# Keys and queries of the later head pairs: through a scratch in device memory into float32r tiles, and transposed as float32r

## The chip, the cores and the metric

The kernel runs on one core of one Trainium2 chip. The core has five engines with instruction streams of their own: PE (matrix products, with its weight loads listed as PEld), DVE, ACT, POOL and SP; in this kernel SP issues nearly all transfers. Each engine takes its instructions in the order of the program and waits on semaphores for the others. The metric is device microseconds for one execution, lower is better; the time quoted is the median of several runs.

## The reference, cut to what matters

The program is an attention block and two dense blocks behind it. Only the first is touched here.

```python
# q, k, v: (2, 8, 768, 64) float32, proj: (64, 6)
q_bits = (np.einsum('bhsd,dk->bhsk', q, proj) > 0).astype(np.int64)
k_bits = (np.einsum('bhsd,dk->bhsk', k, proj) > 0).astype(np.int64)
q_bucket = np.sum(q_bits * powers, axis=-1)
k_bucket = np.sum(k_bits * powers, axis=-1)
mask = q_bucket[:, :, :, None] == k_bucket[:, :, None, :]
scores = scale * np.matmul(q, k.transpose(0, 1, 3, 2))
scores = np.where(mask, scores, -1000000000.0)
attn = softmax(scores)                       # written out in the original
x = np.matmul(attn, v)                       # -> (1536, 512) tokens
x = np.maximum(np.maximum(x @ w1, x @ w2), x @ w3) @ w_out
out = gelu_sigmoid(x @ w_in) @ w_out2        # widths 2048 and 512
```

## The kernel before, in words

The 16 heads are taken as 8 pairs `g` (two heads of one batch side by side). For each pair the kernel loads k, q and v (`load_raw`, tiles `raw`, three buffers), and brings k and q into a layout with the feature on the partition by transposing 128x128 blocks on PE against an identity (`prep_transpose`, L293, into a PSUM tile `T`): 2 tensors x 2 halves x 3 blocks, 12 transposes for a pair. ACT and DVE split each transposed half into a high and a low float32r part (`kq`: L302 to L310). Four products of `kq` with the projection give the bucket bits (`prep_bits`, L319; `aug`), and eight transfers per head put it all together as `kst` and `qst` (`prep_stack`, L343).

The first pair goes another way (`load_first`, `solo_transpose` L363, `solo_bits` L392 and L394), with tiles of its own and transposes with 64 columns of weights. `solo_bits` needs `pds`, which DVE makes from `proj` (tile `pf`, loaded by ACT's queue in L1303) in L1312 to L1320.

Then each of 96 units `u` (128 queries of a head) goes through scores (L425, tile `S`), clamp and row minimum on DVE (L432, tile `se`), exponential on ACT (L438), the reciprocal of the sum (L442), scaling on POOL (L448), transposition on PE in float32 (L457), a high and a low part (L463, L467) and the product with v (L475, `PV`). The result is moved by three small transfers (`xm`, `xt`: L500 to L503) and added and split on POOL (L508 to L518). After that come the dense blocks (L681 to L1212), whose products are in float32r.

The order on every engine in the attention part is set by `plan`: a list of tasks with a due time (`u` plus `DUE`), dependencies, buffers taken and given, and an engine with an occupancy and a latency from `COST`. SP is planned like an engine; its kinds are `raw`, `stack`, `xm`, `xm2` and `wraw`. `filled` puts products on zeros (L1483) into PE's gaps of the plan in the first part. The planned order is then enforced on each engine (`in_order`).

Of the kernel before, what the change touches and what calls it, by code (L numbers as in the profile page):

```python
# [201 lines left out]
def build(tc, q, k, v, proj, w1, w2, w3, w_out, m2_in, m2_out, out):  # L202
# [16 lines left out]

    sb_all = tc.tile_pool(name="sb", bufs=1)  # L220
    sb = sb_all.__enter__()
    sb_att = tc.tile_pool(name="sb_att", bufs=1)
    at = sb_att.__enter__()
    ps_att = tc.tile_pool(name="ps_att", bufs=1, space=bass.MemoryType.PSUM)
# [4 lines left out]
    def st(shape, tag, bufs, dtype=F32, pool=None):  # L229
        seq[0] += 1  # L230
        if pool is None:
            pool = sb if tag in shared else at
        return pool.tile(shape, dtype, tag=tag, name=f"{tag}_{seq[0]}", bufs=bufs)
# [21 lines left out]
        nc.tensor.matmul(wps[:, :512], warm[:, :P], warm, start=True, stop=True)  # L255
    ident = st([P, P], "ident", 1)
    make_identity(nc, ident)
    off = st([NR, 1], "off", 1)
    nc.gpsimd.memset(off, 0.0)
    for n, base in enumerate((70, 64, 50, 44, 38, 18, 12, 6)):  # L260
# [16 lines left out]
    stacks = {}  # L277
    vstack = {}

    def load_raw(g, what):  # L280
        b, p = divmod(g, NPAIR)
        for name, src in (("k", k), ("q", q), ("v", v)):
            if name in what:
                t = st([P, NTILE, 2, D], "raw", 3)
                for j in range(2):
                    nc.sync.dma_start(t[:, :, j, :], src[b, 2 * p + j].rearrange("(p c) d -> p c d", c=NTILE))
                qkv_raw[g, name] = t

    def prep_transpose(g, name, a, get):
        t = qkv_raw[g, name]  # L290
        pst = get()
        for c in range(3):
            nc.tensor.transpose(pst[:, c * P:(c + 1) * P], t[:, 3 * a + c].rearrange("p j d -> p (j d)"), ident)  # L293
        if a == 0:
            kq[g, name] = (st([P, S], "kq", 4, F32R), st([P, S], "kq", 4, F32R))
        s = slice(a * HALF, (a + 1) * HALF)
        hi, lo = (x[:, s] for x in kq[g, name])
        o = pst[:, :HALF]

        def on_act():  # L300
            if name == "k":
                nc.scalar.copy(hi, o)  # L302
            else:
                nc.scalar.activation(hi, o, AF.Copy, scale=QSCALE)

        def on_dve():
            if name == "k":
                nc.vector.tensor_tensor(out=lo, in0=o, in1=f32(hi), op=ALU.subtract)
            else:
                nc.vector.scalar_tensor_tensor(out=lo, in0=o, scalar=QSCALE, in1=f32(hi),  # L310
                                               op0=ALU.mult, op1=ALU.subtract)
        return on_act, on_dve
# [979 lines left out]
    if True:  # L1292
# [46 lines left out]
        def task(kind, u, fn, name=None, deps=(), take=(), give=(), cost=None):  # L1339
            tasks.append((u + DUE[kind], len(tasks), fn, name, deps, take, give, COST[cost or kind]))  # L1340
# [17 lines left out]
        task("pd1", 0, project_high, ("pdth",), deps=[("pdf",)], cost="high")  # L1358
        task("pd1", 0, project_low, ("pdt",), deps=[("pdth",), ("sp", 0, 3)], cost="low")
        task("raw", -36, lambda: load_raw(0, "v"), ("r0", "v"))  # L1360
        task("S", -99, lambda: None, ("PE", "warm"), cost="warm")
        task("v", -2, lambda: prep_v(0, 0), ("vs", 0, 0), deps=[("r0", "v")])
        for g in range(NG):
# [4 lines left out]
            task("v", u0, lambda g=g: prep_v(g, 1), ("vs", g, 1), take=("vs",), deps=[("vs", g, 0)],  # L1368
                 give=("rv",))
            if g + 1 < NG:  # L1370
                task("raw", u0, lambda g=g: load_raw(g + 1, "k"), ("rk", g + 1), take=("rk",))
                task("raw", u0, lambda g=g: load_raw(g + 1, "q"), ("rq", g + 1), take=("rq",))
                task("raw", u0 + 8, lambda g=g: load_raw(g + 1, "v"), ("rv", g + 1), take=("rv",))
                task("v", u0 + 9, lambda g=g: prep_v(g + 1, 0), ("vs", g + 1, 0), take=("vs",), deps=[("rv", g + 1)])
                for n in range(6):
# [110 lines left out]
            t[2]()  # L1486
        ps_att.__exit__(None, None, None)
        sb_att.__exit__(None, None, None)
        moe_jobs()
        in_order(first)  # L1490
    sb_all.__exit__(None, None, None)
# [29 lines left out]
```

## Time and profile before

| what | value |
|---|---|
| median of 3 runs | 674.24 us (674.07 to 674.43) |
| the profiled execution, its time | 674.57 us |
| its span, from the first to the last instruction | 672.8 us |
| PE busy | 666.1 us (99%) |
| DVE busy | 570.1 us (85%) |
| ACT busy | 438.3 us (65%) |
| POOL busy | 320.2 us (48%) |

The span is 1.8 us shorter than the time of the same execution, and that execution is 0.33 us above the median. Busy time of PE counts overlapping products as one stretch and includes the draining of each, so PE at 99% is not PE at its peak: how long a product occupies PE is read from the distance between starts.

### The profile page before, as it was taken

How to read it: one execution, taken by the hardware profiler on the slowest of the kernel's cores; microseconds unless marked ns; L12 is line 12 of the kernel's file. 1: busy time of each engine (PE TensorE's matmuls, PEld its weight loads, DVE VectorE, ACT ScalarE, POOL GpSimd, SP SyncE). 2: the span in 40 equal slices, each digit the busy share in tenths (PEclk: the TensorE clock that was granted, in tenths of full speed). 3: DMA queues.
4: the chain of work that ended last, by engine and by line, in shares of the span. 5: the costliest groups of instructions: out<-in, count | busy, mean ns of one | idle time of the engine just before them, and what ended most of it. 6: DMA issues, size and time to landing. Idle time of an engine off the chain costs nothing.

```text
span 672.8 us, 11441 instructions
## 1 busy us (share of the span) xinstructions
PE 666.1 (99%) x3931; PEld 586.6 (87%) x3933; DVE 570.1 (85%) x1052; ACT 438.3 (65%) x882; POOL 320.2 (48%) x425
## 2 busy tenths in 40 slices
PE   8999999999999999999999999999999999999998
PEld 6899999999999988888888888888888888888886
DVE  8999988999999859999998878886878878787945
ACT  6999989899999835455554554787363736546360
POOL 7476777887887743723433052222333434242400
PEclk9999999999999999999999999999999999999999
DMA  4767578676846112222222132131312130212005
GB/s 117 158 150 174 133 167 195 153 179 139 197 111 144 29 47 64 63 63 64 63 90 67 48 111 93 34 96 62 95 45 80 63 95 31 94 33 94 33 1 188
DMA packets 73690, 64.96 MB, mean 97 GB/s; under 512 B 38608, under 2 KB 64464, under 8 KB 73632
## 3 DMA queue, kind: packets, MB, share of 16 engines
q1 hardware_dynamic: 73408, 64.10, 36.2%
q8 instruction: 31, 0.51, 0.3%
q14 instruction: 27, 0.22, 0.1%
q10 hardware_dynamic: 224, 0.13, 0.1%
HBM read 38.80 MB, written 3.15 MB: 62 GB/s over the span
## 4 chain that ended last, share of the span: by engine, by line
PE 89%; DVE 3%; POOL 3%; DMA 2%; issue 1%; ACT 1%; POOLq 0%; SPq 0%; ACTq 0%
PE acc L902 33%; PE acc L1201 19%; PE PV L475 8%; PE T L457 7%; PE S L425 7%; PE acc L1061 7%; PE acc L681 4%; PE T L681 1%; DVE se L432 1%; POOL se L448 1%; PE T L319 1%; DMA xm<-xt 1%; PE T L293 1%; DVE ptl L467 1%; DMA xt<-xt 1%
## 5 line engine op out<-in xcount | busy, mean ns | idle before, releaser
L594 POOL TENSOR_SCALAR wmag<-wmag 128x512 f32<-128x512 f32 (+1 forms) x58 | 45.9, 792 | 122.5 <-ACT wmag L587 122.1
L467 DVE TENSOR_TENSOR ptl<-T,pth 128x512 fp32r<-128x512 f32 x144 | 93.9, 684 | 8.2 <-ACT pth L463 7.8
L448 POOL TENSOR_SCALAR se<-se,rc 128x768 f32<-128x768 f32 x96 | 87.2, 919 | 20.7 <-DVE rc L442 17.2
L432 DVE TENSOR_SCALAR_CACHE_REDUCE se<-S 128x768 f32<-128x768 f32 x96 | 90.3, 948 | 3.8 <-PE S L425 3.4
L438 ACT ACTIVATE se<-se,mn 128x768 f32<-128x768 f32 x96 | 91.1, 951 | 2.3 <-DVE se L432 2.2
L425 PE MATMUL S<-kst,qst 128*128 128x512 f32 (+3 forms) x384 | 87.7, 354 | 0.2 <-DVE se L432 0.2
L463 ACT CAST pth<-T 128x512 fp32r<-128x512 f32 x144 | 78.0, 592 | 5.9 <-PE T L457 4.9
L457 PE MATMUL T<-ident,se 128*128 128x128 f32 x576 | 77.5, 273 | 1.3 <-POOL se L448 0.6
L1201 PE MATMUL acc<-wolo,gh 128*128 128x512 f32 (+1 forms) x194 | 75.0, 387 | 0.0
L1201 PE MATMUL acc<-wohi,gh 128*128 128x512 f32 (+1 forms) x194 | 75.0, 387 | 0.0
L475 PE MATMUL PV<-pth,vst 128*128 128x256 f32 x288 | 73.6, 290 | 0.0
L475 PE MATMUL PV<-ptl,vst 128*128 128x256 f32 x288 | 71.2, 282 | 0.0
L457 PEld LDWEIGHTS T<-ident,se 128*128 128x128 f32 x576 | 65.6, 140 | 4.3 <-POOL se L448 1.1
L1209 DVE TENSOR_TENSOR res<-acc,res 128x512 f32<-128x512 f32 (+1 forms) x85 | 57.3, 682 | 11.1 <-PE acc L1201 9.0
L425 PEld LDWEIGHTS S<-kst,qst 76*128 76x128 f32 (+1 forms) x384 | 59.0, 190 | 6.3 <-DVE se L432 1.4
L1201 PE MATMUL acc<-wohi,gl 128*128 128x512 f32 (+1 forms) x194 | 59.3, 387 | 0.0
L622 POOL TENSOR_TENSOR wlo<-wmag,whi 128x512 fp32r<-128x512 f32 (+1 forms) x28 | 37.8, 1350 | 39.8 <-ACT whi L617 39.7
L475 PEld LDWEIGHTS PV<-pth,vst 128*128 128x128 f32 x288 | 54.7, 190 | 1.3
L475 PEld LDWEIGHTS PV<-ptl,vst 128*128 128x128 f32 x288 | 54.9, 191 | 0.0
L902 PE MATMUL acc<-xl,whi 128*128 128x256 f32 (+1 forms) x150 | 47.1, 327 | 0.0
L902 PE MATMUL acc<-xh,whi 128*128 128x256 f32 (+1 forms) x150 | 46.9, 326 | 0.0
L617 ACT CAST whi<-wmag 128x512 fp32r<-128x512 f32 (+1 forms) x42 | 25.3, 601 | 27.3 <-DVE wmag L612 24.0
(236 smaller groups left out, 1724.1 us busy)
## 6 DMA issues: line engine op xcount, KB each, us to landing
wraw<-in_moe_w_dram SPq DMA_DIRECT2D x18, 512.0 KB, 4.4
wraw<-in_moe_w_in_dram SPq DMA_DIRECT2D x16, 512.0 KB, 3.8
wraw<-in_moe_w_out_dram SPq DMA_DIRECT2D x16, 512.0 KB
kst<-kq SPq DMA_DIRECT2D x42, 192.0 KB, 3.5
qst<-kq SPq DMA_DIRECT2D x42, 192.0 KB, 3.5
raw<-in_k_dram SPq DMA_DIRECT2D x16, 192.0 KB, 3.2
raw<-in_q_dram SPq DMA_DIRECT2D x16, 192.0 KB, 3.8
raw<-in_v_dram SPq DMA_DIRECT2D x16, 192.0 KB, 4.2
```

The lines of the kernel that those rows point to most:

```text
L425: nc.tensor.matmul(pss[:, x], qs[r, k, c * P:(c + 1) * P], ks[r, k, x], start=k == 0, stop=k == 1)
L432: nc.vector.tensor_scalar(out=se[u], in0=pss[:, :S], scalar1=1.0e9, scalar2=None, op0=ALU.min, op1=ALU.min, accum_out=mn[u])
L438: nc.scalar.activation(se[u], se[u], AF.Exp, bias=mn[u], scale=-1.0, accum_out=sm[u // 2][:, u % 2:u % 2 + 1])
L448: nc.gpsimd.tensor_scalar(out=se[u], in0=se[u], scalar1=rc[u // 2][:, u % 2:u % 2 + 1], scalar2=1.0, op0=ALU.mult, op1=ALU.mult)
L457: nc.tensor.transpose(pst[:, i * P:(i + 1) * P], se[2 * jq + o][:, c * P:(c + 1) * P], ident)
L463: nc.scalar.copy(ptr[jq][0][:, n * 512:(n + 1) * 512], tps[jq, n])
L467: nc.vector.tensor_tensor(out=ptr[jq][1][:, s], in0=tps[jq, n], in1=f32(ptr[jq][0][:, s]), op=ALU.subtract)
L475: nc.tensor.matmul(pv[jq], vs[:, c, :], ptr[jq][t].rearrange("p (o c n) -> p c o n", o=2, c=NTILE)[:, c], start=(c == 0 and t == 0), stop= ...
L902: nc.tensor.matmul(o, w[:, c], x[:, c], start=first and m == 0, stop=m == len(turns) - 1, skip_group_check=True)
L1061: nc.tensor.matmul(o, w[:, c % 3, :], h[:, s], start=(c == 0 and z == 0), stop=(c == FT - 1 and z == 2))
L1201: nc.tensor.matmul(o, g[:, s], w.rearrange("p c f -> p (c f)")[:, e], start=n == 0, stop=n == len(turns) - 1)
L1209: nc.vector.tensor_tensor(out=res[t][:, e], in0=o, in1=res[t][:, e], op=ALU.add)
```

## The change

A pool in device memory is opened (`dr_att`), and for pairs 1 to 7 a new task `move_raw` copies k and q (2 heads, 384 KB each) from the input to a scratch tile there, two buffers for each name. `load_raw` then reads k and q from the scratch, into a `raw` tile that is declared float32r (the bits are those of the float32 input). v is loaded as before. The transposes of `prep_transpose` take this tile and a float32r copy of the identity, `identr`, and write PSUM through a float32r view. The first pair and the transposes of L457 stay float32. The costs in `COST` and the due times in `DUE` are unchanged.

```diff
     sb = sb_all.__enter__()
+    dr_att = tc.tile_pool(name="dr_att", bufs=1, space=bass.MemoryType.DRAM)
+    dr = dr_att.__enter__()
...
     make_identity(nc, ident)
+    identr = st([P, P], "identr", 1, F32R)
+    nc.scalar.copy(identr, ident)
...
+    def move_raw(g):
+        b, p = divmod(g, NPAIR)
+        for name, src in (("k", k), ("q", q)):
+            moved[g, name] = dr.tile([2, S, D], F32, tag="moved" + name, name=f"moved_{name}{g}", bufs=2)
+            nc.sync.dma_start(moved[g, name], src[b, 2 * p:2 * p + 2])
...
-                t = st([P, NTILE, 2, D], "raw", 3)
+                t = st([P, NTILE, 2, D], "raw", 3, F32 if name == "v" else F32R)
                 for j in range(2):
-                    nc.sync.dma_start(t[:, :, j, :], src[b, 2 * p + j].rearrange("(p c) d -> p c d", c=NTILE))
+                    x = src[b, 2 * p + j] if name == "v" else moved[g, name][j]
+                    nc.sync.dma_start((t if name == "v" else f32(t))[:, :, j, :], x.rearrange("(p c) d -> p c d", c=NTILE))
...
-            nc.tensor.transpose(pst[:, c * P:(c + 1) * P], t[:, 3 * a + c].rearrange("p j d -> p (j d)"), ident)
+            nc.tensor.transpose(pst[:, c * P:(c + 1) * P].bitcast(F32R), t[:, 3 * a + c].rearrange("p j d -> p (j d)"), identr)
...
+        task("raw", -35, lambda: move_raw(1), ("moved", 1))
...
-                task("raw", u0, lambda g=g: load_raw(g + 1, "k"), ("rk", g + 1), take=("rk",))
-                task("raw", u0, lambda g=g: load_raw(g + 1, "q"), ("rq", g + 1), take=("rq",))
+                task("raw", u0, lambda g=g: load_raw(g + 1, "k"), ("rk", g + 1), take=("rk",), deps=[("moved", g + 1)])
+                task("raw", u0, lambda g=g: load_raw(g + 1, "q"), ("rq", g + 1), take=("rq",), deps=[("moved", g + 1)])
+                if g + 2 < NG:
+                    task("raw", u0 + 7, lambda g=g: move_raw(g + 2), ("moved", g + 2))
```

The first place is the beginning of ACT's program, which the copy of the identity enters. Before (`pf` is the tile for `proj`, `kst` the first high part of pair 0):

```order
L1303 DMA pf_95<-in_proj_dram 64x6
L370 ACT_TABLE_LOAD
L370 CAST kst_109<-T_130 64x384
L370 CAST kst_109<-T_134 64x384
L372 ACTIVATE qst_110<-T_139 64x384
```

And with the change (L383 and L385 are the old L370 and L372):

```order
L261 ACT_TABLE_LOAD
L261 CAST identr_79<-ident_74 128x128
L1316 DMA pf_99<-in_proj_dram 64x6
L383 CAST kst_113<-T_134 64x384
L383 CAST kst_113<-T_138 64x384
```

The table load and the copy of the identity now stand ahead of the issue of the transfer of `proj`, which was ACT's first work.

The second place is SP in the middle of the attention part, where v of pair 4 and k and q of pair 5 are loaded. Before (`xm` and `xt` are the small moves of a result, `wraw` a block of dense weights):

```order
L503 DMA xt_336_1440<-xt_380_1627 64x256
L286 DMA raw_1690<-in_v_dram 128x6x64 x2
L568 DMA wraw_1710<-in_moe_w_dram 128x4x256
L286 DMA raw_1727<-in_k_dram 128x6x64 x2
L502 DMA xm_1503<-xt_413_1742 64x256
L503 DMA xt_352_1502<-xt_413_1742 64x256
L286 DMA raw_1774<-in_q_dram 128x6x64 x2
```

And with the change (L299 loads into `raw`, L290 fills the scratch, L515 and L516 are the old L502 and L503):

```order
L516 DMA xt_337_1463<-xt_381_1650 64x256
L299 DMA raw_1713<-in_v_dram 128x6x64 x2
L581 DMA wraw_1733<-in_moe_w_dram 128x4x256
L290 DMA moved_k_1743<-in_k_dram 16x6144
L290 DMA moved_q_1745<-in_q_dram 16x6144
L299 DMA raw_1772<-moved_k_1184 128x6x64 x2
L515 DMA xm_1526<-xt_413_1766 64x256
L516 DMA xt_353_1525<-xt_413_1766 64x256
```

Two transfers of 384 KB for a later pair stand in front of the load of k and of the small moves `xm` and `xt`.

The third place is PE at the start, around the first transposes of pair 1 (`S` is a tile of scores, `L392` and `L394` are bits of pair 0, `warm` is filling). Before:

```order
L394 MATMUL T_242<-kst_111,pds_98 76x384
L293 MATMUL T_247<-ident_72,raw_179 128x128 x3
L425 MATMUL S_255<-kst_109,qst_110 128x512
L425 MATMUL S_255<-kst_109,qst_110 128x256
L425 MATMUL S_255<-kst_109,qst_110 128x512
L425 MATMUL S_255<-kst_109,qst_110 128x256
L293 MATMUL T_265<-ident_72,raw_179 128x128 x3
L392 MATMUL T_273<-kst_111,pds_98 76x384
```

And with the change, up to the first of them (five fills, of which two rows stand here):

```order
L438 MATMUL S_264<-kst_113,qst_114 128x256
L405 MATMUL T_278<-qst_116,pds_102 76x384
L407 MATMUL T_278<-qst_116,pds_102 76x384
L405 MATMUL T_282<-qst_116,pds_102 76x384
L407 MATMUL T_282<-qst_116,pds_102 76x384
L1499 LDWEIGHTS warm_66
L1499 MATMUL PV_205<-warm_66 128x512
L306 MATMUL T_301<-identr_79,raw_222 128x128 x3
```

The transposes of k of pair 1 come after the fourth tile of scores, the last bits of pair 0 and five fills, no longer around the fourth tile of scores; the transposes of q of pair 1 follow behind the fifth and the sixth tile.

## Rows read from the trace of the kernel before

**Rows 1.** The page: span, busy time of each engine.

```profile
span 672.8 us, 11441 instructions
PE 666.1 (99%) x3931; PEld 586.6 (87%) x3933; DVE 570.1 (85%) x1052; ACT 438.3 (65%) x882; POOL 320.2 (48%) x425
```

**Rows 2.** Chain of waits, first 40 us: start, length, engine, line, count.

```profile
21.61 1.42 PE T L319 x8
...
28.45 1.43 PE PV L475 x12
29.89 1.31 PE T L457 x12
...
36.07 1.41 PE S L425 x8
```

**Rows 3.** Line L293: count, duration in ns (min/median/max), first and last start.

```profile
L293 PEld LDWEIGHTS T<-ident,raw x84: 137/140/143, 12.5 to 187.1; 128*128 128x128 f32 x84
L293 PE MATMUL T<-ident,raw x84: 270/272/328, 12.7 to 187.2; 128*128 128x128 f32 x84
```

**Rows 4.** Stretches: length, busy PE, PEld, DVE, ACT, POOL, PEclk, DMA share, GB/s.

```profile
150.00:200.00 50.00, 48.83 (x372) 46.37 (x371) 47.62 (x102) 46.60 (x100) 41.75 (x60) 1.00 0.64 149
```

**Rows 5.** The same view as rows 4, one stretch of the start.

```profile
20.00:30.00 10.00, 10.00 (x70) 9.20 (x71) 10.00 (x24) 9.32 (x20) 4.30 (x7) 1.00 0.79 172
```

**Rows 6.** Line L319, the same columns as for L293.

```profile
L319 PEld LDWEIGHTS T<-kq,pdt x56: 186/188/192, 21.3 to 190.3; 128*128 128x128 f32 x56
```

**Rows 7.** Timeline of PE: start, length, line, out<-in, weights, moving operand, count.

```profile
11.32 0.49 PE L363 MATMUL T<-ident,raw 128*64 128x128 f32 x3
...
12.70 0.49 PE L293 MATMUL T<-ident,raw 128*128 128x128 f32 x3
```

**Rows 8.** Timeline of ACT at the start; in brackets the idle time before and its end.

```profile
0.80 0.55 ACTq L1303 DMA_DIRECT2D pf<-in_proj_dram  x1
1.39 1.28 ACT L370 ACT_TABLE_LOAD   x1 [1.39 <-PEq L1506]
4.25 0.47 ACT L370 CAST kst<-T 64x384 fp32r<-64x384 f32 x1 [1.58 <-PE T L363]
...
10.07 0.30 ACT L1330 CAST pdt<-pdf 128x128 fp32r<-128x128 f32 x1
```

**Rows 9.** Timeline of POOL at the start.

```profile
1.07 0.29 POOL masks.py:199 TENSOR_SCALAR_AFFINE_SELECT ident<-ident 128x128 f32<-128x128 f32 x1
```

**Rows 10.** Timeline of DVE at the start.

```profile
3.44 0.17 DVE L1312 COPY pf<-pf 64x6 f32<-64x6 f32 x1 [0.62 <-DMA pf<-in_proj_dram]
...
4.75 1.19 DVE L381 TENSOR_TENSOR kst<-T,kst 64x384 fp32r<-64x384 f32 x2 [0.20 <-ACT kst L370]
...
16.04 1.02 DVE L308 TENSOR_TENSOR kq<-T,kq 128x384 fp32r<-128x384 f32 x2
```

**Rows 11.** Timeline of SP's queue at the start: issues of transfers, start and length.

```profile
7.94 1.23 SPq L286 DMA_DIRECT2D raw<-in_k_dram  x2
...
27.03 0.86 SPq L343 DMA_DIRECT2D qst<-aug  x1
```

**Rows 12.** The page, transfers: count, KB of one, us from issue to landing.

```profile
wraw<-in_moe_w_dram SPq DMA_DIRECT2D x18, 512.0 KB, 4.4
...
kst<-kq SPq DMA_DIRECT2D x42, 192.0 KB, 3.5
```

**Rows 13.** Timeline of SP's queue, the second place of the change.

```profile
101.68 0.64 SPq L568 DMA_DIRECT2D wraw<-in_moe_w_dram  x1
...
103.77 2.19 SPq L502 DMA_DIRECT2D xm<-xt  x1
```

**Rows 14.** Timeline of POOL behind it.

```profile
108.91 0.74 POOL L508 TENSOR_TENSOR xt<-xt,xm 128x256 f32<-128x256 f32 x1 [2.23 <-DMA xt<-xt]
```

**Rows 15.** Groups by line: count, busy us, mean ns, idle before and its ends.

```profile
L508 POOL TENSOR_TENSOR xt<-xt,xm 128x256 f32<-128x256 f32 x24 | 18.2, 756 | 11.0 <-DMA xm<-xt 6.0 <-DMA xt<-xt 4.3
```

More of the change, by code (lines that the diff above doesn't have):

```diff
@@ L278, in build @@
     vstack = {}
+    moved = {}
+    def move_raw(g):
[3 more added lines that the diff above has]
+            nc.sync.dma_start(moved[g, name], src[b, 2 * p:2 * p + 2])
     def load_raw(g, what):
@@ L1488, in build @@
         sb_att.__exit__(None, None, None)
+        dr_att.__exit__(None, None, None)
         moe_jobs()
```

## The prediction

> **What bounds the kernel now.** The page comes first: PE is busy for 666.1 of 672.8 us [rows 1], so nothing is short that PE does not do. Busy time of PE counts overlap, so I read next, in the chain of waits, how far apart PE's instructions start: 12 transposes of L457 take 1.31 us, 109 ns each; 12 products of 256 columns (L475) 1.43 us, 119 ns each; 8 products of 384 columns (L319) 1.42 us, 178 ns each [rows 2]. These are pieces in which PE follows PE without a gap. The 84 transposes that the change touches have the same form as those of L457 (272 ns for one, drained) and run from 12.5 to 187 us [rows 3]; at 109 ns they hold PE for 9.2 us, 1.4% of the span. That is the whole stock from which a gain can come.
>
> Then the stretches, for who stands next to PE. From 150 to 200 us DVE is busy for 47.6 of 50 us, ACT for 46.6, POOL for 41.8 [rows 4]. A shorter PE soon meets DVE and ACT there. From 20 to 30 us DVE is busy for all of 10.0 us [rows 5]: at the start DVE sets the pace, and PE has fills in its order. So a gain of PE counts only behind the start, and a delay of DVE at the start counts in full. The attention part is where all edits are; the dense blocks behind it are PE's alone and only begin earlier or later.
>
> **The transposes.** The trace has no float32r product with 128 moving columns. From below: a float32r product costs 119 ns at 256 columns and 178 at 384 [rows 2], 59 for 128 columns, so the line gives 60 ns at 128; that saves 49 ns of 109. From above: the weights of a float32r product with 128 columns load for 188 ns [rows 6], those of the float32 transpose for 140 [rows 3]. If the longer load sets the pace, the nearest row with such loads is L475 with 119 ns, 10 ns worse than now. No row is near either end, since this is a transpose in one respect and a float32r product in the other; I take 85, halfway between 60 and the present 109, a saving of 24. The 12 transposes of pair 1 lie at the start, where DVE sets the pace; 72 are left: 72 x 24 ns = 1.7 us. DVE and ACT are busy for 95 and 93% beside them [rows 4], so I let a quarter go to waits on these: **-1.3 us**, with ends at -3.5 (72 x 49 ns, nothing given back) and +0.7 (72 x 10).
>
> Here the Trainium skill speaks against the change. What the trace shows first: three transposes with 64 columns of weights (L363) take 0.49 us, and three with 128 columns (L293) 0.49 us as well [rows 7]; half the weights bought nothing, so in float32 it is the moving side that sets 109 ns. The Trainium skill, "TensorE: Matmul & The Clock Gate", section "LDWEIGHTS (loading the stationary operand)", has a load last by its count of columns, which for 128 gives 107 ns (an estimate by that page's formula). By that rule a row of transposes with 128 columns of weights would stand at its 109 ns in either type, the term would be zero and the sum +2.1; the 64-column rows do not agree with it for float32, and no row shows it for a float32r transpose. Its case is a rival below.
>
> **The start.** The copy `identr` is put ahead of the issue of the transfer of `proj` on ACT. Before, that issue began at 0.80 us and the table load ran from 1.39 to 2.67 [rows 8]; `ident` was ready at 1.36 [rows 9]. DVE waited for `proj` until 3.44 [rows 10], 2.64 us after the issue. Now ACT begins at 0.80 with the table load (1.28 us, to 2.08), and copies the identity; a cast of 128x128 on ACT lasts 0.30 [rows 8], so the issue begins at about 2.4 and DVE has `proj` at 5.0 instead of 3.44: 1.6 us later. Behind that wait stand the little instructions of `pds`, and L381 at 4.75, which had waited 0.20 us for ACT [rows 10]: DVE's chain up to L381 moves from 4.55 to 6.1, and L381 begins **1.4 us** later. ACT's own copy costs nothing: ACT had been waiting for PE until 4.25 [rows 8]. From L381 on DVE works without a pause until 31 us (its timeline; the last ten of these us are in [rows 5]), so the 1.4 us are handed on to the clamps and from there to PE. Ends: 2.0 if the table load stays at 1.39 (issue at 3.0), and 0.4 if the new order gives 1.0 back: the `kq` pair of L308, 1.02 us [rows 10], no longer stands ahead of the clamp of the fourth tile of scores, so the first reciprocal comes that much earlier. I take **+1.4**: the work is only put off, and DVE has it all before the stretch ends.
>
> The first loads: k of pair 1 was issued at 7.94 [rows 11], when its buffer came free. Now SP must first see the scratch written. Four transfers of 384 KB go out from 4 us on; one of 512 KB lands after 4.4 us [rows 12], so the first is there at about 8.5 and costs nothing, but the other three, 1152 KB, are queued ahead of the load. Between the rows of 192 and of 512 KB lie 320 KB and 0.9 us [rows 12], so 1152 KB are some 3.2 us, and the landing goes from about 12 to 15. PE reaches these transposes behind five fills at about 16 us. `kst` and `qst` of pair 1 go out some 3 us later than before; their last issue ended at 27.9 [rows 11], with 3.5 us to land [rows 12] that is 31.4, and the first tile of scores that needs them (the thirteenth in PE's order) began at 36.07 [rows 2]. The cover is 4.7 us; without it the 3 us would count. I take nothing.
>
> **SP and the transfers in the middle.** Each of the pairs 4 to 7 brings two issues on SP (0.6 us each by the `wraw` issue [rows 13], 1.2 us together), mostly where SP waited for a result to move. More counts what is queued behind: at the second place shown, the 768 KB stand ahead of the load of k and of `xm` and `xt`. There already before, with `wraw` and `raw` in front, the issue of `xm` took 2.19 us [rows 13] and POOL then waited 2.23 us for `xt` [rows 14], with the scaling of the next two units behind it and PE's transposes behind that. In all POOL lost 10.3 us on these two [rows 15], and PE hid most of it, since from 150 to 200 us, with its own share of these waits, it idled for 1.2 us [rows 4]. 768 KB are 2.2 us by the difference of those two rows and 6.6 by the whole of the 512 KB row [rows 12]; nearer the first, as transfers follow each other, so 3. The small moves stand behind the new transfers, or one load further back, at four places; at two the wait is likely to reach POOL, as it did in [rows 14]. I take 0.35 us of PE for each of the two, **+0.7**; the ends are 0 (hidden as before) and +3 (3 us at each of the two, half of it handed on to PE). One fill product less in PE's order is worth 0.2 us at most, at the start, where PE waits anyway: nothing.
>
> **The sum.** -1.3 + 1.4 + 0.7 = +0.8 us. The profiled execution took 674.57 us, so 675.4 by its own time; it lies 0.33 above the median, so against 674.24 the forecast is **675.0 us**. 0.2% or 1.35 us is about what a measurement of this kernel can tell from no change, so this counts as no change: the gain at the transposes is paid back at the start.
>
> **The rivals.**
> *One column per tick, and quiet transfers: faster.* Transposes at 60 ns save 3.5 us; with 1.4 at the start and 0.3 for the transfers that is -1.8, 672.4 us. For it: a float32r product scales by 59 ns for 128 columns. Against it: the 188 ns loads, and DVE and ACT near their own limits. It decides when a transpose falls to 67 ns with nothing given back to DVE and ACT (72 x 42 ns less 1.7 is 1.35). 0.17.
> *The change does nothing at PE: slower.* Transposes stay at 109 (or go to 119 with the longer weight load), and what is left is start and transfers: +2.1, 676.3 us (+2.8, 677.0). For it: the longer load, and that both types are moved as 4-byte words; against it the equal pace of 64 and 128 columns. The rule of the Trainium skill on loads, given above, would have it so. 0.23.
> *The scratch holds up POOL: slower.* `xm` and `xt` land 3 us later, POOL holds the scaling, and PE runs out of tiles: +3 for that term and +3.1 in all, 677.3 us. For it: POOL's 2.23 us wait at that very place; against it, PE's 1.2 us of idle time in 50 with such waits about [rows 4]. It decides from 1.3 us of PE on, twice what I took for both places. 0.15.
>
> **How the numbers follow.** The forecast itself has 0.45 (with it the case that the start gives 1.0 back: -1.3 + 0.4 + 0.7 = -0.2, 674.0). Between the cases lie mixtures, so I put faster at 0.18, the same at 0.42, slower at 0.40. The range runs from the fast rival (672.4) to the slowest one (677.3), a little widened at the upper end for two of them together: 672.3 to 677.7. The forecast's own range is 673.4 to 676.2.
>
> **What would show each step.** The transposes of the pairs: two or more triplets in one piece, at 85 ns each; at 60 or 109 a rival is right. The weight load in their rows: 140 or 188 ns. The start: DVE's wait for `proj` ends at about 5.0, L381 begins at about 6.2, and PE's first tile of scores comes 1.4 us later than before. The middle: POOL's waits for `xm` and `xt`, 10.3 us before, go to about 14, and PE has no new gap over 0.5 us behind them. The first load from the scratch is issued between 8 and 10 us. What would make it wrong: a transpose below 67 ns; a start in which DVE catches up; or transfers through device memory that land far later than 4.4 us.

## The result, and the profile after

The changed kernel took 680.3 us (679.38 to 680.52, 3 runs) against 674.24: ratio of the means 1.0086, 95% interval 1.0063 to 1.0109, so 6.1 us slower, where 675.0 with an upper end of 677.7 was forecast. In a second measurement, beside its variants, it took 678.43 us (677.74 to 679.97, 5 runs) against 673.89, ratio 1.0067 (1.0054 to 1.0080), 4.5 us slower. Both agree on the sign; how they differ comes out below. One run of new_order_early_copy, a kernel told of below, took 1347.58 us, twice the others, and is left out of its figures.

The page of the profiled execution (680.3 us), the lines that answer to [rows 1]:

```profile
span 678.6 us, 11457 instructions
PE 668.6 (99%) x3931; PEld 586.0 (86%) x3932; DVE 570.6 (84%) x1052; ACT 438.6 (65%) x883; POOL 319.7 (47%) x425
```

No engine has noticeably more to do: the 5.8 us of span came in as waiting or as slower work. First the transposes, by their line (the answer to [rows 3]):

```profile
L306 PEld LDWEIGHTS T<-identr,raw x84: 137/140/144, 18.2 to 191.0; 128*128 128x128 f32 x84
L306 PE MATMUL T<-identr,raw x84: 222/248/409, 18.2 to 191.0; 128*128 128x128 f32 x84
...
  DVE ptl L480: 2.1, 7
  DVE kq L321: 1.0, 4
```

The last two lines say what PE waited for ahead of them: us in all, times. Before, the same view of L293 had:

```profile
  DVE ptl L467: 0.5, 2
  DVE kq L308: 0.2, 1
```

The weight load stayed at 140 ns, and one transpose fell from 272 to 248 ns, drained. How far apart they start is seen in the chain of waits, where PE follows PE:

```profile
161.33 0.74 PE T L306 x9
```

That is 82 ns each, and 85 ns is the median distance of two starts on this line: the assumed 85. It is a mixture: 22 of the 84, mostly the first two of a piece, have the next start behind them after 58 to 67 ns, 44 after 78 to 93. But PE now waits 3.1 us ahead of them for DVE to release their tiles; before it was 0.7 us. Counted from the start of each transpose to that of PE's next product, waits included, the 84 take 9.31 us, before 9.25: against before, nothing was gained on this line.

Now the start. Engine by engine (ACT, DVE, PE; in brackets the idle time before and what ended it):

```profile
0.80 1.28 ACT L261 ACT_TABLE_LOAD   x1 [0.80 <-PEq L1523]
1.41 0.59 ACTq L1316 DMA_DIRECT2D pf<-in_proj_dram  x1
2.09 0.30 ACT L261 CAST identr<-ident 128x128 fp32r<-128x128 f32 x1
...
5.03 0.30 DVE L1325 COPY pf<-pf 64x6 f32<-64x6 f32 x1 [2.18 <-DMA pf<-in_proj_dram]
...
6.75 1.02 DVE L394 TENSOR_TENSOR kst<-T,kst 64x384 fp32r<-64x384 f32 x2
...
7.35 0.60 PE L405 MATMUL S<-kst,pds 128*76 128x384 f32 x1 [1.23 <-DVE kst L394]
7.75 0.52 PE L407 MATMUL S<-kst,pds 128*76 128x384 f32 x1
8.07 0.84 PE L376 MATMUL T<-ident,raw 128*64 128x128 f32 x3
...
11.82 1.75 PE L438 MATMUL S<-kst,qst 128*128 128x512 f32 x8
```

The first tile of scores before:

```profile
9.38 1.75 PE L425 MATMUL S<-kst,qst 128*128 128x512 f32 x8
```

DVE has `proj` at 5.03 us, as predicted, but by another way: ACT's queue issued the transfer at 1.41, ahead of the copy, not at 2.4. So only 0.6 us of the 1.6 are the later issue; landing took 3.6 us from it instead of 2.6, now with the first loads of k and q issued ahead of it (a likely reason that no run tests by itself). L394 begins 2.0 us later than L381 did, and PE's first tile of scores at 11.82 instead of 9.38. The rows from 7.35 to 8.07 hold one thing that no step foresaw: a triplet of transposes takes 0.84 us, where [rows 7] have 0.49.

The first load from the scratch, in the timeline of SP's queue:

```profile
10.22 1.27 SPq L299 DMA_DIRECT2D raw<-moved_k  x2
```

And the stretch of [rows 4], with the same columns:

```profile
150.00:200.00 50.00, 48.03 (x356) 44.44 (x356) 45.71 (x98) 44.65 (x96) 39.98 (x58) 1.00 0.71 162
```

From 150 to 200 us PE did less than before (356 products, not 372) and idled for 2.0 us instead of 1.2; as the kernel is some 5 us late there, it is not quite the same work.

To see where the time goes I read in PE's timeline when certain of the 96 tiles of scores begin, in each profiled execution. Before: 1st at 9.38 us, 13th 35.91, 33rd 80.89, 49th 120.45, 61st 148.16, 93rd 219.02. The difference to that, in us (the other kernels are told of below):

| kernel | 1st | 13th | 33rd | 49th | 61st | 93rd |
|---|---|---|---|---|---|---|
| changed | +2.43 | +2.63 | +3.32 | +3.67 | +5.08 | +5.32 |
| changed, second measurement | +1.57 | +1.74 | +2.81 | +3.23 | +4.66 | +4.43 |
| late_identity | -0.01 | +0.17 | 0.00 | -0.14 | +1.41 | +1.16 |
| new_order_alone | -0.43 | -0.22 | -0.09 | -0.21 | +1.53 | +1.49 |
| new_order_and_moves | -0.01 | +0.20 | +0.49 | +0.46 | +2.11 | +2.23 |
| new_order_early_copy | +1.62 | +1.80 | +1.91 | +1.81 | +3.53 | +3.34 |
| changed_float32_transposes | +1.57 | +1.75 | +1.89 | +1.94 | +3.51 | +3.33 |
| before_with_early_copy | +1.56 | +1.55 | +1.55 | +1.55 | +1.55 | +1.07 |
| moves_in_old_order | -0.19 | +2.17 | +2.08 | +4.33 | +4.51 | +3.80 |
| transposes_alone | -0.25 | -0.27 | -0.51 | -0.59 | -0.49 | -1.42 |
| late_by_other_work | +3.02 | +4.87 | +4.69 | +4.49 | +6.07 | +5.83 |

A delay is carried through: most rows stay within 0.1 to 0.3 us between two columns, over 40 us and more. So each larger step in a row is a place. From the 93rd tile to the first product of the dense blocks the kernels with the new order lose 0.3 to 0.4 us more (there the changed one has +5.75, late_identity +1.55, new_order_alone +1.85); behind that no more than 0.2 us is lost or won.

### The profile page after: what moved, and what is told of

It reads as the page before. It is cut to its first block, busy times and chain, and to the rows that moved or that the text cites. A ratio compares the mean times of both kernels' runs of the same rounds, so it can differ in the third digit from the quotient of the medians.

```text
span 678.6 us, 11457 instructions
## 1 busy us (share of the span) xinstructions
PE 668.6 (99%) x3931; PEld 586.0 (86%) x3932; DVE 570.6 (84%) x1052; ACT 438.6 (65%) x883; POOL 319.7 (47%) x425
## 4 chain that ended last, share of the span: by engine, by line
PE 88%; DVE 3%; ACT 3%; DMA 2%; POOL 2%; issue 1%; SPq 0%; DVEq 0%; POOLq 0%; ACTq 0%
PE acc L915 32%; PE acc L1214 19%; PE PV L488 8%; PE S L438 7%; PE acc L1074 7%; PE T L470 7%; PE acc L694 4%; ACT se L451 1%; PE T L694 1%; DVE ptl L480 1%; PE T L332 1%; DVE se L445 1%; ACT pth L476 1%; DMA xt<-xt 1%; POOL se L461 1%
## 5 line engine op out<-in xcount | busy, mean ns | idle before, releaser
L1214 PEld LDWEIGHTS acc<-wolo,gh 128*128 128x128 f32 x194 | 36.4, 188 | 7.5
```

What stands on the lines that cost most here:

```text
L1214: nc.tensor.matmul(o, g[:, s], w.rearrange("p c f -> p (c f)")[:, e], start=n == 0, stop=n == len(turns) - 1)
```

## The experiments

The theory after the first reading had three causes: the late start (A), the new order that the planner made on PE, DVE, ACT and POOL because SP had more tasks (B), and transfers that land later (C). The first four kernels part them.

**late_identity.** The copy goes behind the issue of `proj`.

```diff
-    nc.scalar.copy(identr, ident)
...
         nc.scalar.dma_start(pf[0:D, 0:6], proj)
+        nc.scalar.copy(identr, ident)
```

> The changed kernel, with the copy of the identity put behind the issue of the transfer of proj on ACT; all else is as changed. Theory A (the start): PE's first tile of scores comes 2.4 us later in the changed kernel because DVE gets proj late, and nothing behind gives it back; then DVE has proj at 3.4 us as before, the first tile of scores begins at about 9.4 us, and the time is 680.3 - 2.4 = 677.9 us. Rival: the start is taken up later by PE's waits for DVE and ACT, and the time stays at 680.0 us or above.

676.14 us against 674.34, ratio 1.0027 (1.0017 to 1.0037), where 677.9 was expected. DVE has `proj` again as before:

```profile
3.35 0.17 DVE L1325 COPY pf<-pf 64x6 f32<-64x6 f32 x1 [0.53 <-DMA pf<-in_proj_dram]
```

Against the first measurement the early copy was worth 4.2 us, more than the 2.4 seen at the start; against the second, each beside its own runs of before, 2.7 us.

**moves_in_old_order.** All the scratch traffic, but not as tasks of the planner.

```diff
-        task("raw", -35, lambda: move_raw(1), ("moved", 1))
-                    task("raw", u0 + 7, lambda g=g: move_raw(g + 2), ("moved", g + 2))
...
+        if "v" in what:
+            for n in ((1, 2) if g == 0 else (g + 2,)):
+                if n < B * NPAIR:
+                    move_raw(n)
```

> Late identity; the scratch transfers are issued together with the loads of v, outside the list of tasks, so that every engine but SP has the order of the kernel before; the transposes are float32r. It has all the traffic of the change and none of the new order. Theory B (order): the loss of some 3.5 us behind the start, and the 1.7 us that the transposes should have saved on top, come from the new order on PE, DVE and ACT; then this kernel shows the transposes' gain, 674.2 - 1.7 = 672.5 us. Theory C (traffic): the loss comes from transfers that land later, and this kernel takes 677.9 us, as with the late identity alone.

677.55 us, ratio 1.0045 (1.0032 to 1.0057): theory C for this order. The view of waits has both places, up to 38 us and from 105 to 123 us (total, times, longest):

```profile
PE T L309 <- DMA raw<-moved_k: 1.7, 1, 1.7
...
POOL xt L524 <- DMA xt<-xt: 5.0, 1, 5.0
```

This is the rival in which the scratch holds up POOL: 2.23 us of [rows 14] became 5.0, and the row in the table steps by 2.2 there. The 2.4 us up to the 13th tile are not that wait of 1.7 us alone: behind it PE's granted clock was 0.66 from 15 to 20 us.

**before_with_early_copy.** The kernel before and the early copy, which nothing reads.

```diff
     make_identity(nc, ident)
+    identr = st([P, P], "identr", 1, F32R)
+    nc.scalar.copy(identr, ident)
```

> The kernel before with nothing added but the copy of the identity into a float32r tile (which nothing reads) ahead of the issue of the transfer of proj. Theory A: the first tile of scores comes 2.0 to 2.4 us later and the time is 676.2 to 676.6 us. By the step of the prediction it is 1.4 us, 675.6 us. Rival: the delay comes from the scratch transfers of the start and not from the copy, and the time is within 0.5 us of 674.2.

676.7 us (675.55 to 677.85), ratio 1.0037 (1.0025 to 1.0049). Its chain of waits shows the mechanism: the transfer takes 3.63 us, and DVE's small steps stand behind it.

```profile
0.79 0.61 ACT L259
1.40 3.63 DMA pf<-in_proj_dram
...
5.05 0.28 DVE pf L1314
```

In the profiled execution (675.66 us) the shift is 1.55 us from the first tile on: the predicted term of 1.4, nearly. The median has 2.4, and it is a mixture: the three executions with a mean clock of 1.0 took 675.55 to 676.25, the three with 0.995 to 0.997 took 677.16 to 677.85.

**new_order_alone.** The scratch tasks are planned and do nothing; loads are direct, transposes float32, the copy late.

```diff
     def move_raw(g):
-        b, p = divmod(g, NPAIR)
...
+        pass
...
-                    x = src[b, 2 * p + j] if name == "v" else moved[g, name][j]
+                    x = src[b, 2 * p + j]
```

> The changed kernel's order on PE, DVE, ACT and POOL, with the tasks for the scratch kept in the planning but issuing nothing: loads come from the inputs, the transposes are float32, the identity is copied late. Theory B (order): some 3.5 us more than before at the dense blocks, and no gain of the transposes, so 677.9 + 1.7 = 679.6 us, and new waits of PE for T tiles in the middle. Theory C (traffic): without the scratch transfers nothing is lost, 674.2 us within 0.5.

676.2 us, ratio 1.0030 (1.0019 to 1.0040): between the two theories, with B right in kind and its size missed by 3.4 us. The order by itself costs 1.9 us without one byte moved to the scratch, nearly all of it between the 49th and the 61st tile. SP's loads stand in the new order as well here, so the run does not part SP's order from that of the other engines.

**new_order_and_moves.** The late identity with float32 transposes.

```diff
-            nc.tensor.transpose(pst[:, c * P:(c + 1) * P].bitcast(F32R), t[:, 3 * a + c].rearrange("p j d -> p (j d)"), identr)
+            nc.tensor.transpose(pst[:, c * P:(c + 1) * P], t[:, 3 * a + c].rearrange("p j d -> p (j d)"), ident)
```

> The changed kernel with the late identity, and its transposes left in float32: new order and scratch traffic, without the float32r transposes. It stands between two runs: the new order alone (676.2 us) and the late identity (676.14 us, which has float32r transposes as well). Theory D: the transposes gain 1.3 to 1.7 us as predicted and the traffic eats as much; then this takes 677.4 to 677.9 us. Theory E: the transposes' gain is mostly turned into waits of PE for T tiles (0.3 us is left) and the traffic costs as little in this order, which was planned with it; then 676.2 to 676.5 us.

676.86 us against 674.48, ratio 1.0034 (1.0022 to 1.0046). Against the kernel before in the same runs it is +2.4; the order alone +1.9, the late identity +1.8. So the traffic costs 0.5 us in the order planned with it, and the transposes give back 0.6. That is between the theories, nearer E. PE's waits ahead of the transposes say where the rest went: for `ptl` and `kq` 1.0 + 0.6 us here, 1.9 + 1.0 in the late identity. Of 84 x 24 ns = 2.0 us, 1.3 became waits for DVE. The count from start to start agrees: 9.91 us for the 84 here, 9.20 in the late identity.

**new_order_early_copy.** new_order_alone with the copy early.

> The new order without scratch traffic and with float32 transposes, and the identity's copy ahead of the issue of proj's transfer: what an early copy costs in the new order. In the order of before it cost 2.4 us (676.7 against 674.3), in the changed kernel taking it away saved 4.2 us. Theory F: the new order makes the start itself dearer (PE's clock rises later), and this takes 676.2 + 4.2 = 680.4 us. Theory G: what goes beyond 2.4 us is transfers and small moves falling upon each other when the start is late, and needs the scratch traffic; then this takes 677.8 to 678.6 us.

678.44 us (median of five, 677.66 to 680.76), ratio of the means 1.0065 (1.0050 to 1.0080): in theory G's range. Against new_order_alone, each beside its own runs of before, the early copy costs 2.1 us. The profiled execution took 678.03, 1.6 us of shift at the start and 1.9 of the order, no more: without traffic there are no further steps. The two that took 679.95 and 680.76 have a mean clock of 0.997 and 0.995, the other three 0.999 or 1.0.

**transposes_alone.** The old order; pairs 2 to 7 read one scratch.

```diff
+                    x = src[b, 2 * p + j] if name == "v" or g == 1 else moved[2, name][j]
...
+        if (g, what) == (1, "q"):
+            move_raw(2)
```

> The order of before, the identity copied late, pair 1 as before; the tiles of pairs 2 to 7 are loaded from one scratch that is filled once, from pair 2, at about 12 us, and are transposed as float32r (so pairs 3 to 7 work on the keys and queries of pair 2, and the result is another). Almost no traffic is added, and the 72 transposes that the prediction counted are changed. By the prediction's step: 85 ns each and a quarter lost, 674.3 - 1.3 = 673.0 us; by theory E (PE waits for T tiles instead): 674.0 to 674.3 us.

673.75 us against 674.48, ratio 0.9991 (0.9982 to 0.9999): 0.7 us, half of the predicted 1.3. The line's own view again (PE's waits ahead, us, times):

```profile
  DVE ptl L485: 1.5, 5
  DVE kq L326: 0.4, 1
```

1.9 us where before had 0.7: of the 1.7 us of 72 transposes 1.2 went into new waits.

**cast_loads_on_pool.** No scratch: POOL's transfers convert to float32r, which changes the values of k and q.

```diff
-                    x = src[b, 2 * p + j] if name == "v" else moved[g, name][j]
-                    nc.sync.dma_start((t if name == "v" else f32(t))[:, :, j, :], x.rearrange("(p c) d -> p c d", c=NTILE))
+                    x = src[b, 2 * p + j]
+                    x = x.rearrange("(p c) d -> p c d", c=NTILE)
+                    (nc.sync if name == "v" else nc.gpsimd).dma_start(t[:, :, j, :], x)
```

> No scratch: k and q of pairs 1 to 7 are loaded straight from the inputs into the float32r tiles, by transfers that POOL issues; v stays on SP; order of before but for these issues, the identity copied late. If POOL's 28 issues cost nothing: 674.3 - 1.3 = 673.0 us (by theory E 674.1). Rival: POOL is held at each issue, by its own work on the transfer or by the wait for a free tile, with the scaling behind it, and 28 issues of some 1 us each, half of it handed on in a stretch where POOL is busy for 84%, make it slower than 676 us.

689.69 us, ratio 1.0228 (1.0208 to 1.0247): the rival, more than it said. Each pair of issues holds POOL for 1.7 to 1.9 us, ahead of the scaling that PE waits for:

```profile
21.43 1.69 POOL L299 DMA_DIRECT2D raw<-in_q_dram  x2
23.16 0.92 POOL L461 TENSOR_SCALAR se<-se,rc 128x768 f32<-128x768 f32 x1
```

**late_by_other_work.** The late identity, and DVE busy with 13 more clears.

```diff
-        nc.vector.memset(pdf, 0.0)
+        for _ in range(14):
+            nc.vector.memset(pdf, 0.0)
```

> The late identity (676.14 us) with 13 more clears of a small tile on DVE, 0.17 us each, ahead of its work on proj: DVE reaches proj some 1.7 us later, as in the changed kernel, by another cause and with the transfer of proj in its old place. The changed kernel lost 2.4 us at its start and 1.7 us more behind it; without scratch traffic the same early copy lost nothing more behind the start. Theory G (a late start and the scratch traffic together make small moves land too late for POOL): 1.6 to 2.4 us at the start and 1 to 1.7 us behind it, 679 to 680.3 us. Rival: what is lost behind the start belongs to the transfers of the early copy itself; then this is 677.8 to 678.5 us, with the shift constant from the first tile of scores on.

681.36 us, ratio 1.0105 (1.0092 to 1.0118). The time is 1.1 us above theory G's range, and the reason is another: the shift is 4.87 us at the 13th tile and from there follows the late identity to within 0.2. Nothing more is lost behind the start in this execution, so a late start and the traffic are not enough for the steps at 80 and 120 us; below, a kernel with its start in time has them, so a late start is not needed either: theory G falls. What made the start so dear is the clock (stretches; the last but two numbers: PEclk):

```profile
10.00:15.00 5.00, 4.22 (x15) 3.12 (x14) 3.91 (x7) 1.97 (x5) 3.50 (x10) 0.50 0.52 143
15.00:20.00 5.00, 4.93 (x24) 3.52 (x25) 3.95 (x9) 2.95 (x6) 3.20 (x6) 0.85 0.34 76
```

**one_product_pair_later** and **values_prepared_later** look for the place where the new order loses time. In new_order_alone PE waits at 148 us for ACT to copy the one PSUM tile PV:

```profile
148.52 0.39 PE L484 MATMUL PV<-pth,vst 128*128 128x256 f32 x1 [0.85 <-ACT xt L502]
```

The first puts these products behind the next tiles, as before; the second also puts a preparation of v on POOL behind two scalings, as before.

```diff
+        x = order.pop(names.index(("PV", 27, 0)))
...
+        n = names.index(("T", 28, 2)) + 1
+        order.insert(n, (order[n - 1][0], x[1]))
...
+        x = order.pop(names.index(("vs", 5, 0)))
...
+        n = names.index(("w", 1, 1)) + 1
```

> The late identity (676.14 us) with one piece of PE's order put back: the first six products with v of query group 27, which the new order has directly behind those of group 26, go behind the next transposes and two tiles of scores, where the order of before has them. Theory: PE waits 1.0 us at 147 us because the only PSUM tile PV is not yet copied out by ACT, and this single place is half of what the new order costs; then 675.1 to 675.3 us. Rival: the wait only moves on to the next tile that DVE and ACT have not released, and the time stays within 0.3 us of 676.1.

> The late identity with two pieces of the order of before put back: the products with v of group 27 (as in the run before, which only moved PE's wait to POOL's scaling: 1.37 us) and, on POOL, the preparation of v of pair 5 (1.6 us) behind the two scalings that PE waits for at 147 us instead of ahead of them. Theory: this place on POOL is what the new order costs there, 1.0 to 1.4 us; 674.8 to 675.3 us. Rival: DVE's reciprocal and ACT hold the next tiles, and it stays at 676 us.

676.85 us (1.0040, 1.0028 to 1.0052) and 676.03 us (1.0031, 1.0020 to 1.0042). Both theories missed, and both rivals have the mechanism, though the first kernel took 0.45 us more than its rival allowed. The wait moved on, first to POOL's scaling, which had the preparation of v ahead of it,

```profile
148.86 0.66 PE L469 MATMUL T<-ident,se 128*128 128x128 f32 x4 [1.37 <-POOL se L460]
...
146.31 0.51 POOL L420 TENSOR_SCALAR vst<-raw 128x384 fp32r<-128x384 f32 x1
146.90 1.02 POOL L422 TENSOR_TENSOR vst<-raw,vst 128x384 fp32r<-128x384 f32 x1
147.90 1.79 POOL L460 TENSOR_SCALAR se<-se,rc 128x768 f32<-128x768 f32 x2
```

and then, with that out of the way, to the reciprocal on DVE, which POOL now waits for:

```profile
148.11 1.79 POOL L460 TENSOR_SCALAR se<-se,rc 128x768 f32<-128x768 f32 x2 [0.90 <-DVE rc L454]
```

The median hides that something came back: between the 49th and the 63rd tile the profiled execution of the second kernel lost 1.0 us, that of the late identity 1.5; PE's wait for POOL was down from 1.37 to 0.59 us. It lost 0.9 us before the 33rd tile and 0.5 before the 49th instead, in steps that are told of below. So no single place holds the 1.9 us; they arise in a stretch where DVE, ACT and POOL stand at 95, 93 and 84% beside PE [rows 4]. Which changes of the order would bring them back stays open.

**five_pairs_old_order** and **moves_on_pool** try for a version faster than both: old order, pairs 1 and 6 left as before, or pair 1 as before and the rest moved by POOL.

```diff
+    DIRECT6 = (1, 6)
...
-            nc.sync.dma_start(moved[g, name], src[b, 2 * p:2 * p + 2])
+            nc.gpsimd.dma_start(moved[g, name], src[b, 2 * p:2 * p + 2])
```

> The order of before, identity late; pairs 2, 3, 4, 5 and 7 go through the scratch (pair 2 moved behind the loads of pair 1, the others behind the load of v), pairs 1 and 6 are loaded and transposed as before. These two are the ones whose transfers cost something when all went through the scratch in the old order: PE waited 1.7 us for pair 1, POOL 5.0 us for a small move behind pair 6. With 60 float32r transposes the gain should be 60/72 of the 0.7 us of the transposes alone: 674.3 - 0.6 = 673.7 us. Rival: the waits turn up at another pair, 675 us or more.

> The order of before, identity late; pair 1 as before, pairs 2 to 7 through the scratch, whose 12 filling transfers are issued by POOL and stand in another queue than the small moves. If what costs is the place in SP's queue, POOL no longer waits 5 us for a small move, and the time is 674.3 - 0.7 = 673.6 us. If what costs is the traffic itself, small moves land as late as in the old order with all moves on SP: 676 us or more. POOL's own time for 12 issues at 0.85 us each, measured where it issued the loads, can add up to 2 us in the stretches where POOL is busy for 84%.

674.16 us (1.0004, 0.9995 to 1.0012) and 676.05 us (1.0032, 1.0019 to 1.0044). The first is no different from the kernel before, as if the transposes' gain paid for the traffic and no more. In the second, at the place where POOL waited 5.0 us with the moves on SP, it still waits 3.6:

```profile
111.03 0.74 POOL L527 TENSOR_TENSOR xt<-xt,xm 128x256 f32<-128x256 f32 x1 [3.60 <-DMA xt<-xt]
```

So, by one execution of each, most of what costs there is not the place in SP's queue. The Trainium skill, "DMA: Bandwidth & Descriptors", section "Queues, rings and completion order", has each DMA engine take turns between its queues packet by packet; a wait that falls from 5.0 to 3.6 us and does not vanish is in line with that, and no run here shows the turns themselves.

**changed_again** and **changed_float32_transposes** (the changed kernel with the diff of new_order_and_moves).

> The changed kernel as it is, beside its variants and against the same runs of before. What was shown so far adds up to 4.1 us: new order 1.9, scratch traffic 0.5, transposes -0.7, late start 2.4. The first measurement was 6.1 us. If the missing 1.7 to 2 us belong to the kernel (small moves that land too late whenever its start is late by just this much), it takes 680 us again, with PE losing 0.7 us at 76 to 81 us and 0.5 us at 115 to 120 us. If they belong to that execution's transfers, it takes 678 to 679 us and the shift behind the start stays constant.

> The changed kernel (early copy of the identity, new order, scratch traffic) with its transposes in float32. With the identity late, leaving the transposes in float32 cost 0.7 us (676.86 against 676.14); if terms add, this is 0.7 us slower than the changed kernel of the same runs. Rival: the missing 1.7 us are a matter of where the small moves fall, then another 0.1 us here and there moves them and the difference can have either sign.

678.43 us and 680.99 us (678.18 to 682.04; ratio 1.0095, 1.0079 to 1.0112). The steps at 80 and 120 us are there again in the changed kernel (1.2 and 0.5 us against the late identity; execution of 679.28 us), and in values_prepared_later, with its start in time. They are not in the late identity, in one_product_pair_later or in late_by_other_work, and with float32 transposes there is at most 0.3 us at the first of them. At that first step POOL waits in changed_again for the small moves `xm` and `xt`:

```profile
73.06 0.53 SPq L515 DMA_DIRECT2D xm<-xt  x1
73.63 0.60 SPq L516 DMA_DIRECT2D xt<-xt  x1
...
75.71 2.67 SPq L299 DMA_DIRECT2D raw<-in_v_dram  x2
78.47 1.29 SPq L299 DMA_DIRECT2D raw<-moved_q  x2
...
78.69 0.74 POOL L521 TENSOR_TENSOR xt<-xt,xm 128x256 f32<-128x256 f32 x1 [1.46 <-DMA raw<-moved_k]
```

By the trace's semaphore events `xt` landed at 78.53, 4.9 us after its issue, and POOL went on 0.16 us later; the load that the row names landed only at 78.89. The two issues of v, which took 2.67 us, stand behind these moves, so they are not what held them. In the late identity the moves landed sooner, `xt` at 74.25, 3.8 us after its issue; the two issues of v took 1.68 us, and POOL did not wait:

```profile
69.91 0.53 SPq L514 DMA_DIRECT2D xm<-xt  x1
70.48 0.60 SPq L515 DMA_DIRECT2D xt<-xt  x1
...
72.88 1.68 SPq L298 DMA_DIRECT2D raw<-in_v_dram  x2
...
75.51 0.74 POOL L520 TENSOR_TENSOR xt<-xt,xm 128x256 f32<-128x256 f32 x1
```

In the first measurement's execution `xt` landed 5.0 us after its issue and in values_prepared_later 5.2. At the second step POOL waits for `xt` in all of them, and longer where there is a step: 1.82, 1.68 and 1.79 us in changed_again, the first measurement's execution and values_prepared_later, 1.28 and 1.20 in the late identity and late_by_other_work. So with the scratch traffic an execution may or may not lose these 1.3 to 1.7 us; why the same moves take an extra microsecond in some stays open.

The second kernel took 2.6 us more than changed_again, which contradicts "terms add". Its start varies: four of its six executions took 680.7 us or more with a mean clock of 0.995, the other two 678.2 and 678.7 at 0.999 and 1.0.

## Why the prediction was wrong

The sum was -1.3 + 1.4 + 0.7 = +0.8. Measured, each term against before in its own runs: transposes -0.6 to -0.7, start +1.6 in executions where the clock rises in time and 2.1 to 2.7 in the medians, traffic +0.5, and a term that was not in the sum, **the new order, +1.9**. With the start at 1.6 that gives +3.4, or 677.3 us by the runs of before beside changed_again; its two fastest executions took 677.74 and 677.75.

**The step that failed** is that on SP and the transfers in the middle, with its last sentence: it priced the change of order as what is queued on SP and as one fill less, "nothing". The order was changed on all engines. The trace of before could not price that, but it told how little room there was (DVE 95%, ACT 93%, POOL 84% beside PE), and the order of the changed kernel was to be had: an unknown term, without a lower bound of zero, that belonged into the range. Of the 5.3 us between the forecast of 675.0 and the measured 680.3 the order is the largest part, 1.9; the late clock at the start, the transposes and the steps at 80, 120 and 198 us, told of below, make up most of the rest. With 1.9 us more the range would have held the second measurement with room, and still not quite the first.

**The transposes.** 85 ns was right as a median (82 in a piece without waits), the weight load of 140 ns too; halfway between 60 and 109 was luck, since the starts are a mixture of some 60 and some 85 ns. The quarter given to waits was too little: 1.2 of 1.7 us went there. The rival in which loads set the pace is wrong: starts 82 ns apart are closer than one load of 140 ns is long. The Trainium skill, "TensorE: Matmul & The Clock Gate", section "LDWEIGHTS (loading the stationary operand)", gives 107 ns for a load of 128 columns (an estimate by its formula); the trace's 140 ns are longer, and its 82 ns between starts shorter. In the rival of the faster transposes 72 x 42 ns less 1.7 is 1.3, not 1.35; nothing hangs on it.

**The start.** Size and place were right (5.03 us; L394 2.0 us later: 1.6 by `proj`, 0.6 by small steps of DVE that lasted up to 0.40 us instead of 0.17, less the 0.2 that L381 had waited for ACT), the way was not: the issue moves by 0.6 us, the landing by 1.0 more, so that 5.0 us came out was luck. The gain of the new order at the start (0.4 us in new_order_alone) is real and smaller than the 1.0 taken for the low end. What was missed is PE's clock (below).

**The first loads.** Issued at 10.22, just behind the 8 to 10 us that were named, and hidden in the new order, as taken. In the old order they are not: PE waited 1.7 us.

**The scratch and POOL.** The rival had the right mechanism and its price, 677.3 us, for a kernel that was not run: in the old order it happens (5.0 us, 677.55). In the changed kernel the planner knew of the moves; 0.5 us is left, and POOL's waits for `xm` and `xt` were 10.4 us up to 240 us (9.0 before, in the same view), where 14 were forecast. On top of it come 1.3 to 1.7 us in some executions.

**The first measurement.** Between the profiled executions of before and after lie 680.30 - 674.57 = 5.7 us, and that of before was 0.33 above its median. Of the 5.7, 2.4 are the start (1.6, and 0.85 for the half clock), 1.6 what the late identity has at the end of the attention part (order, traffic and transposes together), and 1.7 steps at 80, 120 and 198 us. That these 1.7 us are small moves that land later, with POOL waiting for them, is seen at the first two places; for the third, and for why some executions have them, it stays open.

## What to carry to other kernels

A planner makes a new program out of a small change: price the order by running it with the new tasks empty, before any gain inside an instruction is counted. A shorter instruction on the engine that bounds a kernel is worth only what its neighbours can follow; where they are at 95%, a third of it was left. Look at what is put ahead of the first transfers: a copy of 0.30 us that nobody waits for cost 1.6 us and more.

## What the runs showed of the hardware

- **PE's clock at the start.** In the changed kernel's first execution a triplet of transposes still took 0.84 us at 8.07 and at 9.35 us; the starts in a triplet are some 210 ns apart. In changed_again the same rows, behind the same pause (1.23 and 1.24 us), are shorter, with starts 109 ns apart:

```profile
7.36 0.40 PE L405 MATMUL S<-kst,pds 128*76 128x384 f32 x1 [1.24 <-DVE kst L394]
7.59 0.34 PE L407 MATMUL S<-kst,pds 128*76 128x384 f32 x1
7.77 0.49 PE L376 MATMUL T<-ident,raw 128*64 128x128 f32 x3
```

  The column PEclk shows 1.00 in both, so the low level (1.2 of 2.4 GHz) at the start is read from the distances. It made 0.85 us between two executions of one program.
- **A clock that falls again.** With a pause of 2.35 us in PE at the start (late_by_other_work) the clock rose, and fell at about 9.6 us to 0.50 for the stretch from 10 to 15 us; moves_in_old_order had 0.66 from 15 to 20 us, behind a stretch with PE busy for 3.25 of 5 us.
- **An issue on ACT's queue does not wait for ACT's work ahead of it.** With table load and copy first in ACT's program, the transfer was issued at 1.41 us, while the table load ran until 2.08 and the copy from 2.09. It was 0.6 us later than before all the same: POOL finished `ident`, which the copy ahead of it reads, at 1.36, and the issue came 0.05 us behind that.
- **Float32r transposes.** 82 ns apart at 128 columns in a piece of nine (the first two starts 60 to 63, the others 85 to 88), where float32 has 109 [rows 2], with the same weight load of 140 ns; float32r products with 128 columns of weights load for 188 [rows 6].
